# A gated recurrence followed by a low-rank mixer and an MLP: whole-batch loads, two chunks at a time, and fp32 weights cast on chip

## The chip, the cores and the metric

The kernel runs on one core of one Trainium2 chip. Its time is device microseconds of one execution, taken as the median of several runs. The profile is of a further execution, recorded by the hardware profiler. Six instruction streams matter: PE (TensorE, matmuls, with its weight loads PEld beside them), ACT (ScalarE), DVE (VectorE), POOL (GpSimd), and the queues from which transfers are issued, SP (SyncE) and POOL's own. All transfers run on the same 16 DMA engines.

## The reference

There are 4 batches, 8 heads, a sequence of 768 and a head of 48 columns; q, k, v and alpha are float32. Each head carries a state of 48 x 48 along the sequence:

```
state = alpha[t][:, None] * state + outer(k[t], v[t])
y[t]  = q[t] @ state
```

The heads' y, side by side, are x (768 x 384 for a batch), and then

```
xt = x.transpose(0, 2, 1)
h  = xt @ U @ V                        # U: 768 x 32, V: 32 x 768
u  = x + h.transpose(0, 2, 1)
out = u + relu(u @ w_ch1) @ w_ch2      # w_ch1: 384 x 1536, w_ch2: 1536 x 384
```

## The kernel before

Nothing is scheduled at run time. `Plan.add` collects operations, each with an engine, a cost in ns, what it reads and writes (`r`, `w`) and a priority. `Plan.run` then plays them through with those costs: at each step, of the operations that could start first, it takes the one with the lowest priority number, gives its `Buf`s the slot of their `Pool` that comes free first, and calls its function, which emits the instructions. So the order of each engine's stream is fixed when the kernel is built, and an engine that meets an instruction whose data is late waits with all that stands behind it.

The recurrence is computed by chunks of 128 steps, six to a batch, for all 8 heads at once (`stage_gla`, once per chunk). Heads go in four pairs, one of a pair on partitions 0 to 47 and the other from 64 on. The steps of a chunk, with their lines:

- four loads of 128 x 8 x 48 float32 from SP (L263): alpha, k, q, v, one chunk each, from a pool `io` of 40 slots. The innermost run in memory is one head's row of 48 numbers, 192 bytes;
- ACT takes the log of alpha into `lt` (L265), POOL casts v to bf16, `rv` (L267);
- PE forms the cumulative sum with a triangle of ones (L272) and its totals by head pair (L274);
- ACT takes exp of minus the sum, `ai` (L282), of the sum, `aa` (L283), and of the totals, `tot` (L284);
- POOL multiplies: `rk` = k times `ai` (L286), `rq` = q times `aa` (L287);
- PE transposes the four head pairs of each (L295), ACT (L304) and DVE (L306) copy them out of PSUM into `qk`;
- PE forms the scores (L321), DVE multiplies them with a triangular mask into `pm` (L332), once for each half of the heads;
- PE forms y from the state (L347) and from the masked scores (L352), and ACT copies it into `xb` (L363);
- PE adds the old state (L376) and the products of k and v (L381), DVE scales the sum with `tot` into the next state `st` (L389).

`stage_mix` does the low-rank part of a batch: x with U (L406), a copy (L414), V with that (L417), the sum into `ub` (L418), transposes (L427) and their copies into `uT` (L435). `mlp1` has two halves of 384 columns, 12 tiles of three products each (L447), with relu on ACT (L455) and DVE (L457) in turn. `mlp2` has, for each of the six chunks, 12 products (L471), the sum into `ou` (L478) and a store (L479).

The weights come by POOL's queue, cast to bf16 by the transfer: U (L245), four copies of V (L247), w_ch1 (L250) and w_ch2 (L253). The first two are issued behind the first chunk, the others behind the fourth and the fifth chunk of batch 0.

PSUM has eight banks: two pairs for scores and y (`pair`), two single ones (`gen`), and two for the MLP (`mlp`). The last batch's MLP may use all of them.

Of the kernel before, what the change touches and what calls it, by code (L numbers as in the profile page):

```python
# [14 lines left out]
class Pool:  # L15


    def __init__(self, slots):
        self.slots = list(slots)
        self.free = [0.0] * len(self.slots)  # L20


class Buf:


    def __init__(self, pool=None, slot=None):
        self.pools = pool if isinstance(pool, list) else ([pool] if pool else [])
        self.slot = slot
        self.home = None
        self.idx = 0  # L30
        self.left = 0
        self.last = 0.0
# [5 lines left out]
class Op:  # L38
    __slots__ = ("eng", "cost", "fn", "prio", "deps", "bufs", "n", "end", "users", "est", "i", "keep")


class Plan:


    LAT = {"PE": 230.0, "ACT": 120.0, "DVE": 120.0, "POOL": 150.0, "SP": 0.0, "DMA": 0.0}

    def __init__(self):
        self.ops = []
        self.writer = {}
        self.readers = {}  # L50

    def add(self, eng, cost, fn, r=(), w=(), prio=0.0, keep=(), after=()):
# [4 lines left out]
        op.keep = keep  # L57
# [14 lines left out]
        op.deps.update(x for x in after if x is not None)  # L72
        op.deps.discard(op)
        bufs = []
        for k in list(r) + list(w) + list(keep):
            b = k[0] if isinstance(k, tuple) else k
            if isinstance(b, Buf) and b not in bufs:
                bufs.append(b)
        op.bufs = bufs
        for b in bufs:  # L80
            b.left += 1
# [3 lines left out]
    def run(self):  # L85
# [12 lines left out]
        while todo:  # L98
            best = None
            for eng, cand in ready.items():  # L100
                now = clock.get(eng, 0.0)
                ok = []
                for op in cand:
                    t = op.est
                    for b in op.bufs:
                        if b.slot is None:
                            s = [x for p in b.pools for x in p.free if x is not None]
# [15 lines left out]
            for b in op.bufs:  # L123
                if b.slot is None:
                    _, n, x = min((f, n, x) for n, p in enumerate(b.pools) for x, f in enumerate(p.free) if f is not None)
                    p = b.pools[n]
                    p.free[x] = None
                    b.home, b.idx, b.slot = p, x, p.slots[x]
# [9 lines left out]
            for b in op.bufs:  # L138
                b.left -= 1
                b.last = max(b.last, op.end + self.LAT[eng])  # L140
                if b.left == 0 and b.home is not None:
                    b.home.free[b.idx] = b.last
# [18 lines left out]
def kernel(  # L161
# [22 lines left out]
    W = 112  # L184
    TW = S // 2

# [22 lines left out]
    vm_sb = const.tile([128, S], BF16, name="vm_sb")  # L209

    io = Pool(slots("io", 40, [C, H, D], FP32))
    lt_s = slots("lt", 3, [C, H, 64], BF16)
# [318 lines left out]
```

## Time and profile before

| | |
|---|---|
| median of 3 runs (lowest, highest) | 210.85 us (210.44, 213.79) |
| the profiled execution | 212.57 us |
| its span, first to last instruction | 210.8 us |
| mean granted TensorE clock | 0.992 |
| busy: PE / DVE / ACT / POOL | 174.7 / 97.4 / 91.3 / 60.8 us |
| read from HBM, written | 24.08 MB, 4.72 MB |
| packets under 512 bytes, of all | 101104 of 106244 |

The profile's page cuts the span into 40 equal slices and gives for each the busy tenths of an engine, the share of the DMA engines and what they moved in GB/s. A row of the timeline has a start and a duration in us, the engine, the line, the operation and the tiles (output, arrow, inputs), how many, and in brackets how long the engine stood idle before and what ended that. A row of the windows has a stretch and its length, then the busy time of PE, PEld, DVE, ACT and POOL (with the number of instructions), the granted clock, the DMA share and GB/s. A row of a chain has a start, a duration, and what the time was spent on. A row of the groups has, after the bar, the total busy time, the mean ns of one, and the idle time before the group with what ended it. Matmuls are pipelined and their ends modelled, so PE's busy time is more than its work.

### The profile page before, as it was taken

What the parts mean: (1) busy time and instruction counts of PE and PEld (TensorE: products, weight loads), DVE (VectorE), ACT (ScalarE), POOL (GpSimd) and SP (SyncE); (2) the same over time, 40 slices, a digit from 0 to 9 for tenths busy, and PEclk for the clock granted to TensorE, in tenths of its full rate; (3) what the DMA queues carried; (4) which work ended last, traced back from release to release, by engine and by line L of the source; (5) the groups of instructions that cost most, each with busy time, mean ns of one, the idle gap of its engine ahead of it and who ended that gap; (6) DMA issues with size and microseconds to landing.
All of it is one profiled execution on the core that took longest, in us unless ns stands there. A gap on an engine that the chain in (4) does not pass through costs nothing.

```text
span 210.8 us, 4417 instructions
## 1 busy us (share of the span) xinstructions
PE 174.7 (83%) x1732; PEld 107.5 (51%) x1732; DVE 97.4 (46%) x196; ACT 91.3 (43%) x209; POOL 60.8 (29%) x92
## 2 busy tenths in 40 slices
PE   1367868204899999899998499999999999999993
PEld 0245646001656655465665356565465656566561
DVE  1124526002657564766646557565542544433331
ACT  3255454003586654967465744643341450320100
POOL 8544663200074454435462830420000000000000
PEclk9999999999999999999999969999999999999999
DMA  7999999999999999999999950011102001212222
GB/s 127 179 188 190 165 190 178 189 190 173 192 168 197 164 195 156 198 174 196 171 212 159 222 164 2 3 37 37 40 0 99 13 3 37 75 40 75 75 74 77
DMA packets 106244, 26.48 MB, mean 126 GB/s; under 512 B 101104, under 2 KB 105840, under 8 KB 106224
## 3 DMA queue, kind: packets, MB, share of 16 engines
q1 hardware_dynamic: 103296, 23.60, 63.5%
q0 software_dynamic: 2928, 2.61, 7.8%
q8 instruction: 13, 0.21, 0.4%
q14 instruction: 7, 0.06, 0.1%
HBM read 24.08 MB, written 4.72 MB: 137 GB/s over the span
## 4 chain that ended last, share of the span: by engine, by line
PE 57%; DMA 16%; SPq 14%; ACT 3%; issue 3%; DVE 3%; POOL 1%; POOLq 0%; ACTq 0%
PE ps L471 21%; PE ps L447 20%; SPq L263 14%; DMA io<-in_alpha_dram 11%; DMA io<-in_v_dram 4%; PE ps L295 3%; PE ps L321 3%; PE ps L352 2%; PE ps L347 2%; DMA out_dram<-ou 2%; PE ps L427 2%; PE ps L417 2%; DVE ub L418 1%; PE ps L381 1%; PE ps L272 1%
## 5 line engine op out<-in xcount | busy, mean ns | idle before, releaser
L447 PE MATMUL ps<-uT,w_sb 128*128 128x384 bf16 x288 | 54.9, 329 | 0.5 <-ACT h1t L455 0.4
L471 PE MATMUL ps<-w_sb,h1t 128*128 128x384 bf16 x288 | 51.9, 326 | 0.0
L455 ACT ACTIVATE h1t<-ps 128x384 bf16<-128x384 f32 x48 | 23.4, 491 | 38.7 <-PE ps L447 38.6
L332 DVE TENSOR_TENSOR pm<-ps,maskc 128x512 bf16<-128x512 f32 x48 | 31.5, 685 | 18.8 <-PE ps L321 18.7
L471 PEld LDWEIGHTS <-h1t 128*128 128x128 bf16 x288 | 26.8, 97 | 16.4 <-issue 0.2
L447 PEld LDWEIGHTS <-w_sb 128*128 128x128 bf16 x288 | 26.2, 98 | 16.6 <-issue 2.2
L457 DVE TENSOR_SCALAR h1t<-ps 128x384 bf16<-128x384 f32 x48 | 26.2, 555 | 16.6 <-PE ps L447 16.0
L286 POOL TENSOR_TENSOR rk<-io,ai 128x384 bf16<-128x384 f32 x24 | 21.9, 913 | 37.6 <-ACT ai L282 35.2
L478 DVE TENSOR_TENSOR ou<-ub,ps 128x384 f32<-128x384 bf16 x24 | 13.3, 553 | 30.8 <-PE ps L471 27.8
L306 DVE COPY qk<-ps 128x512 bf16<-128x512 bf16 x24 | 10.1, 422 | 35.9 <-ACT utx L414 14.6
L265 ACT ACTIVATE lt<-io 128x384 bf16<-128x384 f32 x24 | 12.6, 524 | 32.5 <-DMA io<-in_alpha_dram 32.5
L267 POOL CAST rv<-io 128x384 bf16<-128x384 f32 x24 | 12.1, 503 | 38.6 <-DMA io<-in_v_dram 35.9
L287 POOL TENSOR_TENSOR rq<-io,aa 128x384 bf16<-128x384 f32 x24 | 21.9, 911 | 0.5 <-ACT tot L284 0.3
L304 ACT COPY qk<-ps 128x512 bf16<-128x512 bf16 x24 | 14.0, 583 | 13.0 <-PE ps L295 8.6
L321 PE MATMUL ps<-qk 48*128 48x128 bf16 x192 | 11.2, 247 | 5.3 <-ACT qk L304 3.4
L363 ACT CAST xb<-ps 128x384 bf16<-128x384 f32 x24 | 11.4, 477 | 9.4 <-PE ps L352 9.1
L352 PE MATMUL ps<-rv,pm 128*128 128x48 bf16 x192 | 13.8, 193 | 1.1 <-DVE pm L332 1.0
L282 ACT ACTIVATE ai<-ps 128x384 bf16<-128x384 f32 x24 | 11.9, 494 | 6.0 <-PE ps L274 5.0
L406 PE MATMUL ps<-xb,u_sb 128*32 128x384 bf16 x24 | 3.6, 376 | 12.8 <-ACT xb L363 11.6
L295 PEld LDWEIGHTS <-rq 128*128 128x128 bf16 x96 | 7.1, 108 | 13.6 <-issue 12.4
L418 DVE TENSOR_TENSOR ub<-xb,ps 128x384 bf16<-128x384 bf16 x24 | 12.4, 550 | 3.0 <-PE ps L417 2.6
L272 PE MATMUL ps<-lt,ut_ones 128*128 128x384 bf16 x24 | 9.1, 379 | 5.3 <-ACT lt L265 5.3
(44 smaller groups left out, 164.4 us busy)
## 6 DMA issues: line engine op xcount, KB each, us to landing
io<-in_alpha_dram SPq DMA_DIRECT2D x24, 192.0 KB, 4.5
io<-in_k_dram SPq DMA_DIRECT2D x24, 192.0 KB, 4.6
io<-in_q_dram SPq DMA_DIRECT2D x24, 192.0 KB, 4.4
io<-in_v_dram SPq DMA_DIRECT2D x24, 192.0 KB, 4.5
out_dram<-ou SPq DMA_DIRECT2D x24, 192.0 KB, 1.9
w_sb<-in_moe_w_ch_dram POOLq DMA_DIRECT2D x2, 1152.0 KB, 14.1
vm_sb<-in_moe_V_dram POOLq DMA_DIRECT2D x4, 48.0 KB, 5.2
u_sb<-in_moe_U_dram POOLq DMA_DIRECT2D x1, 48.0 KB, 5.4
```

Source lines behind the costliest of these rows:

```text
L263: P.add("SP", 960, lambda t=t, src=src: nc.sync.dma_start(t(), src[b, :, sl, :].rearrange("h t d -> t h d")), w=[t], prio=kk)
L286: P.add("POOL", 930, lambda: nc.gpsimd.tensor_tensor(rk()[:, :, 0:D], kt(), ai(), op=ALU.mult), r=[kt, ai], w=[rk], prio=pr + 2)
L287: P.add("POOL", 930, lambda: nc.gpsimd.tensor_tensor(rq()[:, :, 0:D], qt(), aa(), op=ALU.mult), r=[qt, aa], w=[rq], prio=pr + 2)
L304: nc.scalar.copy(qk()[:, o : o + HP, :], t[:, o : o + HP, :])
L321: nc.tensor.matmul(s2[:, par, p, :], lhsT=qk()[o : o + D, HP + p, :], rhs=qk()[o : o + D, p, :], start=(p == 0), stop=(p == HP - 1),)
L332: nc.vector.tensor_tensor(pm().rearrange("t (hp two) c -> t two hp c", two=2)[:, par], s2[:, par], maskc.to_broadcast([C, HP, C]), op=ALU. ...
L352: nc.tensor.matmul(y2[:, p, :], lhsT=pm()[:, 2 * p + par, :], rhs=rv()[:, 2 * p + par, :], start=(p == 0 and sprev is None), stop=(p == HP ...
L418: P.add("DVE", 550, lambda c=c, hb=hb: nc.vector.tensor_tensor(ub()[:, c, :], xb()[:, c, :], hb()[:, 0:DM], op=ALU.add), r=[hb, (xb, c)], ...
L447: nc.tensor.matmul(bank(hb)[:, 0:TW], lhsT=w1_sb[:, ct, jt * 128 : (jt + 1) * 128], rhs=uT()[:, ct, tt * TW : (tt + 1) * TW], start=(ct == ...
L455: P.add("ACT", 500, lambda jt=jt, hb=hb: nc.scalar.activation(h1()[:, jt, tt * TW : (tt + 1) * TW], bank(hb)[:, 0:TW], AF.Relu), r=[hb], w ...
L457: P.add("DVE", 560, lambda jt=jt, hb=hb: nc.vector.tensor_scalar_max(h1()[:, jt, tt * TW : (tt + 1) * TW], bank(hb)[:, 0:TW], 0.0), r=[hb] ...
L471: nc.tensor.matmul(bank(hb)[:, 0:DM], lhsT=h1()[:, jt, c * C : (c + 1) * C], rhs=w2_sb[:, jt, :], start=(jt == 0), stop=(jt == NJ - 1),)
```

## The change

- **Loads.** The four inputs come by whole batches (L308): 128 x 48 x 48 float32, 1.18 MB each, in a tile whose rows are 64 numbers wide, so that each run of 48 numbers lies 256 bytes behind the one before. The pool `io` has six such slots. There are 16 loads instead of 96; each still consists of 192-byte runs.
- **Weights.** They no longer come by POOL's queue. U (L275) and four copies of V (L277) are loaded in float32 from SP and cast by POOL (L278, L279). w_ch1 and w_ch2 come in three pieces each (L296), two to an `io` slot, and are cast by ACT or POOL (L270, L272), as a table says.
- **Pairs of chunks.** `stage_gla` works on two chunks at a time: logs, exponentials, products, casts and copies have twice the columns, scores are masked for both halves of the heads at once (L397), and three such steps make a batch. The recurrence over chunks remains: within a step a state is made for each chunk (L422, L429, L432).
- **Engines by hand for batch 0.** For the first batch a table says which engine does the product with k, that with q, the cast of v and the copy of the transposed q; for one chunk of the second and third step ACT copies the scores and POOL cuts the triangle out of them (L301) in place of DVE's mask; and the steps of this batch may also use the MLP's two banks. The later batches have POOL for products and casts, ACT and DVE for the copies.
- **Else.** `ub` is gone: the sum with the low-rank part is written over `xb`. `h1t` has three buffers of half a batch, `uT` two, `ou` three instead of four. The last batch's MLP takes any single bank. The plan's model of a transfer has other numbers.

```diff
-                clock[eng] = t + 450.0
-                dma = max(dma, t + 450.0) + op.cost
-                op.end = dma + 1800.0
+                clock[eng] = max(t + 450.0, dma)
+                dma = max(dma, t + 1200.0) + op.cost
+                op.end = dma + 1700.0
...
-    io = Pool(slots("io", 40, [C, H, D], FP32))
+    io = Pool(slots("io", 6, [C, H * NC, 64], FP32))
...
-    def load_weights():
-        nc.gpsimd.dma_start(u_sb, moe_U.rearrange("(c p) r -> p c r", p=128))
+    def load_low_rank():
+        P.add("SP", 450, lambda: nc.sync.dma_start(u_in, moe_U.rearrange("(c p) r -> p c r", p=128)), w=["u_in"], prio=0.3)
         for g in range(4):
-            nc.gpsimd.dma_start(vm_sb[32 * g : 32 * g + R, :], moe_V)
+            P.add("SP", 250, lambda g=g: nc.sync.dma_start(vm_in[32 * g : 32 * g + R, :], moe_V), w=[("vm_in", g)], prio=0.3)
+        P.add("POOL", 350, lambda: nc.gpsimd.tensor_copy(u_sb, u_in), r=["u_in"], w=["u"], prio=300)
+        P.add("POOL", 1000, lambda: nc.gpsimd.tensor_copy(vm_sb, vm_in), r=[("vm_in", g) for g in range(4)], w=["vm"], prio=300)
...
+        engs = ["ACT", "POOL", "POOL", "ACT", "POOL", "POOL"]
...
+            P.add("SP", 2000, lambda src=src, stage=stage: nc.sync.dma_start(stage(), src), w=[(t, i)], prio=0.5)
+            P.add(engs[i], cost[engs[i]], lambda dst=dst, stage=stage, e=engs[i]: copy(e, dst, stage()), r=[(t, i)], w=[("w1" if i < 3 else "w2", i % 3)], prio=400 + i)
...
+    def load(b):
+        ts = [Buf(io) for _ in range(4)]
+        for t, src in zip(ts, (alpha, k, q, v)):
+            P.add("SP", 4200, lambda t=t, src=src: nc.sync.dma_start(t()[:, :, 0:D], src[b].rearrange("h (c p) d -> p (h c) d", p=C)), w=[t], prio=b)
+        return ts
...
+        first = b == 0
+        win = 3 if first else 2
+        prs = pair0 if first else pair
+        ek = ("POOL", "DVE", "POOL")[g] if first else "POOL"
+        eq = ("DVE", "POOL", "DVE")[g] if first else "POOL"
+        ev = ("ACT", "POOL", "ACT")[g] if first else "POOL"
+        eqt = ("DVE", "DVE", "ACT")[g] if first else "DVE"
+        split = (-1, 1, 1)[g] if first else -1
...
+            if i == split:
+                P.add("ACT", 1150, lambda sc=sc, pmi=pmi: nc.scalar.copy(pmi().rearrange("t two hp c -> t (two hp c)"), sc().rearrange("p two c -> p (two c)")), r=[sc], w=[pmi], prio=pr + 1)
+                P.add("POOL", 1500, lambda pmi=pmi: f_tri(pmi), r=[pmi], w=[pmi], prio=pr + 1)
+            else:
+                P.add("DVE", 1230, f_mask, r=[sc], w=[pmi], prio=pr + 1)
```

What stands where, first on SP. Before, the loads go chunk by chunk (the tile names carry the slot):

```order
L263 DMA io0_82<-in_alpha_dram 128x8x48
L263 DMA io1_83<-in_k_dram 128x8x48
L263 DMA io2_84<-in_q_dram 128x8x48
L263 DMA io3_85<-in_v_dram 128x8x48
L263 DMA io4_86<-in_alpha_dram 128x8x48
```

Now the whole of batch 0 stands first, then the low-rank factors and the weights, then batch 1:

```order
L308 DMA io0_84<-in_alpha_dram 128x48x48
L308 DMA io1_85<-in_k_dram 128x48x48
L308 DMA io2_86<-in_q_dram 128x48x48
L308 DMA io3_87<-in_v_dram 128x48x48
L275 DMA u_in_82<-in_moe_U_dram 128x6x32
L277 DMA vm_in_83<-in_moe_V_dram 32x768 x4
L296 DMA io4_88<-in_moe_w_ch1_dram 128x3x512 x2
L296 DMA io5_89<-in_moe_w_ch1_dram 128x3x512
L296 DMA io5_89<-in_moe_w_ch2_dram 128x4x384
L296 DMA io0_84<-in_moe_w_ch2_dram 128x4x384 x2
L308 DMA io1_85<-in_alpha_dram 128x48x48
```

The first v was the fourth load and had the first chunk's 0.2 MB; it is still the fourth, with the whole batch's 1.18 MB, and the weights stand between the batches.

On DVE, in batch 0. Before, a chunk's masks (`pm`) and its state (`st`) follow one another:

```order
L306 COPY qk0_155<-ps_184 128x512
L389 TENSOR_TENSOR st0_161<-ps_184,tot0_151 112x192
L332 TENSOR_TENSOR pm0_158<-ps_184,maskc_74 128x4x128 x2
L306 COPY qk1_156<-ps_184 128x512
L332 TENSOR_TENSOR pm1_159<-ps_184,maskc_74 128x4x128
```

Now:

```order
L272 COPY qt0_126<-ps_150 128x1024
L272 COPY qt1_127<-ps_150 128x1024
L397 TENSOR_TENSOR pm0_129<-ps_150,maskc_74 128x1024
L397 TENSOR_TENSOR pm1_130<-ps_150,maskc_74 128x1024
L397 TENSOR_TENSOR pm3_132<-ps_150,maskc_74 128x1024
L432 TENSOR_TENSOR st0_133<-ps_150,tot0_119 128x192
L397 TENSOR_TENSOR pm0_129<-ps_150,maskc_74 128x1024
L432 TENSOR_TENSOR st1_134<-ps_150,tot0_119 128x192
```

Three masks of all eight heads stand ahead of the batch's first state, and a fourth ahead of the second.

On POOL, where the last batch begins. Before, it casts one chunk of v (`rv`) in each turn:

```order
L286 TENSOR_TENSOR rk1_129<-io31_113,ai1_150 128x8x48
L287 TENSOR_TENSOR rq2_127<-io32_114,aa1_148 128x8x48
L267 CAST rv0_142<-io4_86 128x384
L286 TENSOR_TENSOR rk2_130<-io30_112,ai0_149 128x8x48
L287 TENSOR_TENSOR rq0_125<-io39_121,aa0_147 128x8x48
```

Now the cast of batch 3's v (the first row of `rv1`, from slot 4) stands ahead of that batch's product with k (slot 3) and with q (slot 5):

```order
L355 TENSOR_TENSOR rq2_95<-io1_85,aa1_114 128x16x48
L272 CAST rv1_111<-io4_88 128x768
L355 TENSOR_TENSOR rk1_97<-io3_87,ai1_117 128x16x48
L355 TENSOR_TENSOR rq0_93<-io5_89,aa0_113 128x16x48
L355 TENSOR_TENSOR rk2_98<-io3_87,ai0_116 128x16x48
```

v is the last of a batch's loads, and the two products of the batch now stand behind its cast.

More of the change, by code (lines that the diff above doesn't have):

```diff
@@ L106, in run @@
                         if b.slot is None:
-                            s = [x for p in b.pools for x in p.free if x is not None]
+                            s = [f for f in map(b.pool.when, range(len(b.pool.slots))) if f is not None]
                             if not s:
@@ L140, in run @@
                 b.last = max(b.last, op.end + self.LAT[eng])
-                if b.left == 0 and b.home is not None:
-                    b.home.free[b.idx] = b.last
+                if b.left == 0:
+                    b.pool.give(b.idx, b.last)
             for u in op.users:
@@ L244, in load_weights @@
[L244 to L263 removed]
+    uts = Pool(slots("uT", 2, [128, NCT, S], BF16))
@@ L368, in stage_gla @@
[L368 to L377 removed]
+                        t[:, i * HP + p, :],
```

408 lines of the change are left out of this document (217 added, 191 removed).

## The prediction

> **What bounds the kernel now.** I read the slices of the page first, then the timeline around the hole in them, then rates by window, and last the chain that ended last.
>
> ```profile
> PE   1367868204899999899998499999999999999993
> DMA  7999999999999999999999950011102001212222
> GB/s 127 179 188 190 165 190 178 189 190 173 192 168 197 164 195 156 198 174 196 171 212 159 222 164 2 3 37 37 40 0 99 13 3 37 75 40 75 75 74 77
> ```
>
> A slice is 5.3 us. PE is loose for ten slices, stands still for one, then is full to the end. The transfers are full from the second slice to the 23rd (some 124 us). So there are two stages: up to 57 us PE waits for data; after it PE works, on what the transfers allow.
>
> ```profile
> 44.59 0.50 POOL L267 CAST rv<-io 128x384 bf16<-128x384 f32 x1 [6.29 <-DMA io<-in_v_dram]
> 49.21 0.52 ACT L265 ACTIVATE lt<-io 128x384 bf16<-128x384 f32 x1 [12.32 <-DMA io<-in_alpha_dram]
> 50.15 0.48 PE L406 MATMUL ps<-xb,u_sb 128*32 128x384 bf16 x1 [11.63 <-ACT xb L363]
> 57.06 0.32 PE L447 MATMUL ps<-uT,w_sb 128*128 128x384 bf16 x1
> ...
> 31.80 8.73 SPq L263 DMA_DIRECT2D io<-in_k_dram  x1
> 40.57 4.86 SPq L263 DMA_DIRECT2D io<-in_q_dram  x1
> 45.48 3.55 SPq L263 DMA_DIRECT2D io<-in_v_dram  x1
> ```
>
> The hole: from 31.8 to 49 us SP is held at three loads in a row (8.73, 4.86 and 3.55 us to issue one) while the weights, casting transfers of POOL's queue, share the 16 transfer engines with them. v of a late chunk comes at 44.6 us, alpha of the next at 49.2, and the MLP of batch 0 (L447) begins only at 57.06.
>
> ```profile
> 2.50:3.25 0.75, 0.00 (x0) 0.00 (x0) 0.00 (x0) 0.00 (x0) 0.75 (x2) 1.00 1.26 255
> 47.00:48.00 1.00, 0.00 (x0) 0.00 (x0) 0.00 (x0) 0.00 (x0) 0.00 (x0) 1.00 1.26 243
> 98.00:99.00 1.00, 1.00 (x17) 0.63 (x14) 0.69 (x2) 0.59 (x3) 1.00 (x2) 1.00 1.25 239
> 99.00:104.00 5.00, 5.00 (x72) 3.26 (x71) 2.60 (x6) 2.52 (x7) 2.90 (x4) 1.00 1.41 190
> 60.00:125.00 65.00, 59.95 (x745) 36.95 (x744) 39.79 (x80) 40.82 (x101) 32.14 (x44) 0.99 1.11 186
> 190.00:200.00 10.00, 10.00 (x63) 6.04 (x62) 3.26 (x6) 0.98 (x2) 0.00 (x0) 1.00 0.22 79
> ```
>
> The last columns are transfer share and GB/s. Loads in 192-byte pieces run at 186 GB/s over a long stretch (190 in a steady part), but at 239 to 255 for about a microsecond after a pause. Stores of 1,536-byte rows moved 79 GB/s at a share of 0.22: 359 GB/s if full.
>
> ```profile
> 161.53 11.70 PE ps L447 x72
> 100.14 0.20 PE ps L352 x4
> 100.86 0.21 PE ps L381 x8
> 103.33 0.33 PE ps L321 x8
> 104.21 0.16 PE ps L272
> 104.38 0.08 PE ps L274 x4
> 107.94 0.22 PE ps L295 x4
> 109.44 0.28 PE ps L406 x4
> 207.40 0.55 DVE ou L478
> 127.00:147.00 20.00, 20.00 (x251) 12.07 (x248) 12.32 (x26) 9.67 (x22) 3.53 (x4) 1.00 0.06 21
> ```
>
> From the chain PE's work can be priced: 0.1625 us for an MLP product (11.70/72), so 23.4 us for a batch's 144; a chunk of the recurrence takes about 2.1 (cumulative sum 0.24, eight transposes 0.45, scores 0.33, y 0.7 to 0.8 at 0.20 for four, state 0.3 to 0.4), the low-rank stage 2.6. In all some 38 us a batch, 151 for four. The stretch from 127 to 147 us has no load left in it and granted clock 1.00; its matmuls, so priced, make 0.95 of the time. The end costs 3.4 us after the last matmul (207.40 to 210.8). The span is 210.8 us, the execution 212.57, the median of the runs 210.85: I sum spans and take them for the median.
>
> **The change, part by part.** Let T be the time of one input tensor of one batch, 1.18 MB. It is the unknown on which nearly all hangs, as the trace has no load in this form (whole batch, rows of 192 bytes put down every 256 bytes). Bounds: 6.3 us at 186 GB/s, 4.6 at 255; outside them 7.2 at the worst busy slice (164), 3.3 at the stores' 359. I take 246 GB/s, the mean of 255, 243 and 239, so T = 4.8: these rows show what the engines do with such pieces, and what seems to push them down, many small transfers, gets rarer (96 loads become 16). That the share is higher (1.41) at 190 than at 239 says that pieces wait for one another when slow. The long row speaks for 6.3 and is kept for the range.
>
> By the Trainium skill, DMA: Bandwidth & Descriptors, "How a descriptor splits into AXI transactions", a piece that does not begin on a 256-byte boundary costs extra beats; rows packed every 192 bytes need 9 beats on average, rows every 256 bytes 6, so if writes are the limit the sum would have 190 x 9/6 = 285 GB/s (estimate from that page), T = 4.1, and end at 182. The trace agrees only in part: packed rows went at 239 too. Against the change speaks the same page's "Specifications": below 512 bytes no line rate, and the pieces stay at 192; by that, T = 6.3 and no gain.
>
> *Batch 0.* The order on SP is alpha, k, q, v, U, V, six weight pieces.
>
> ```profile
> 3.86 0.52 ACT L265 ACTIVATE lt<-io 128x384 bf16<-128x384 f32 x1 [1.85 <-DMA io<-in_alpha_dram]
> L265 ACT ACTIVATE lt<-io 128x384 bf16<-128x384 f32 x24 | 12.6, 524 | 32.5 <-DMA io<-in_alpha_dram 32.5
> L435 ACT COPY uT<-ps 128x768 bf16<-128x768 bf16 x12 | 9.4, 799 | 9.0 <-PE ps L427 9.0
> L286 POOL TENSOR_TENSOR rk<-io,ai 128x384 bf16<-128x384 f32 x24 | 21.9, 913 | 37.6 <-ACT ai L282 35.2 <-PE ps L471 2.3
> L267 POOL CAST rv<-io 128x384 bf16<-128x384 f32 x24 | 12.1, 503 | 38.6 <-DMA io<-in_v_dram 35.9 <-PE ps L295 2.4 <-PE ps L447 0.2
> L332 DVE TENSOR_TENSOR pm<-ps,maskc 128x512 bf16<-128x512 f32 x48 | 31.5, 685 | 18.8 <-PE ps L321 18.7
> L389 DVE TENSOR_TENSOR st<-ps,tot 112x192 bf16<-112x192 f32 x20 | 7.1, 353 | 4.8 <-PE ps L381 4.7
> masks.py:199 POOL TENSOR_SCALAR_AFFINE_SELECT ident<-ident 128x128 bf16<-128x128 bf16 x1 | 0.3, 292 | 0.1
> ```
>
> The first chunk's alpha (0.2 MB, 0.8 us at 246) was in use at 3.86 us: 3.0 us lie around a transfer, and v is there at 3.0 + 4T = 22.2. Logs, exponentials, rk, rq, transposes and scores lie under the loads of k, q and v. After v: the cast of v (0.8, as ACT's 768 columns), three masks that stand ahead of the first state on DVE (2 x 0.685 each, the first about when v lands, 4 us), another mask, five states in a row at about 1.05 each (0.35 on DVE and products and handovers), last y and its copy: some 10 us. Then the low-rank stage, 6.9 us today (50.15 to 57.06): MLP at v + 17, 39 us, against 57.06. The hand-set split keeps other work off this chain: copies on ACT, and a triangle on POOL at between 0.3 and 2.3 us (one or eight of the 128-column row). New are the weight casts: 1,536 columns, 2.0 us on POOL (4 x 0.503), about 1.5 on ACT, four and two of them. One of ACT's stands ahead of two copies of y and is in the 10; POOL's end about when the MLP wants them. If that cover were gone, 2 to 4 us. POOL no longer issues transfers, worth nothing: its queue was not in the chain. The weights are now 4.72 MB at 359 GB/s, 13.1 us, and U and V 1.5; today they take the loads from 32 to 49 us.
>
> *Later batches.* A batch needs four T on the one queue. The slots (six) do not stop it where I follow it: each is read out a few microseconds after landing, the ones for batch 1 while the weights land. v of batch 1 is there at 3.0 + 4T + 14.6 + 4T = 17.6 + 8T; before v of batch 2 come two stores (0.55 each), before v of batch 3 three: 18.7 + 12T and 20.35 + 16T, i.e. 56, 76 and 97 us. These stores wait on DVE with loads behind them on SP, but the loads ahead still keep the engines busy: nothing. Three store buffers for four: nothing, though the third store of batch 0 stands behind v of batch 2 on SP; its buffer is free about 5 us before its next use, and that margin shrinks with nothing but a faster PE.
>
> PE takes its work in a fixed order, so the places where it needs v of a batch matter: in the new order 121, 102 and 80 us of priced work are left there for batches 1, 2, 3. For batch 3: 399 MLP products 64.8, 84 transposes 4.8, scores 2.0, y 3.8, states 1.9, sums 0.5, low rank 2.2. On POOL, the cast of v (1.0) and rk (2 x 0.913) stand between: 2.9 us.
>
> **Sum.** By batch 3: 97.2 + 2.9 + 80.1, 2.0 for PE's loss in the mixed stretch (5% of some 40 us), 3.4 for the end: **186 us**. By PE alone from 39.2: 137.1 of work, 5 lost, 3.4: 185. Both are nearly equal, so a faster T gains 4 us per us of T, a slower one costs 16. The two-chunk tiles halve instructions on ACT, DVE and POOL, which wait on the chain only in batch 0: nothing more.
>
> **The rivals.**
> - *Write-limited rows:* packed rows were what slowed the loads, and they go with the short service of the first row (255 GB/s at a share of 1.26) and as many in flight as the long row has (1.41): 255 x 1.41/1.26 = 285 GB/s, T = 4.1. The kernel is then PE's from batch 0 on: 3.0 + 16.4 + 17 + 137.1 + 5 + 3.4 = 182 us. For it: the share rises while the rate falls, so pieces wait for one another somewhere; against it: the same packed rows at 255. The Trainium skill's count of beats (DMA: Bandwidth & Descriptors), above, speaks for this case.
> - *The new form changes nothing in the rate:* T from 5.4 to 6.65. PE is earlier at the MLP (45 us) and then waits for batches 1, 2 and 3: at 6.3, 20.35 + 100.8 + 88.4 = 210 us; at 5.6, 198. For it: 65 us on end at 186 GB/s, whatever the engines did; against it: no long stretch of one transfer has been seen.
> - *Slower:* whole-batch pieces, 16 engines drifting apart over 48 rows a partition, go no better than the worst slices (164 GB/s), T = 7.2: 20.35 + 115.2 + 88.4 = 224 us. It decides from T = 6.65 on (178 GB/s, 215 us). For it: every third slice shows 154 to 174; against it: the slices beside them make 190.
>
> **How the numbers follow.** T from 4.45 to 5.35 (183 to 194 us): 0.42. Write-limited: 0.25. Unchanged rate: 0.24, of which 0.13 below 206.6 us and 0.11 within 2% (what a measurement here can tell from none). Slower: 0.09. So faster 0.80, same 0.11, slower 0.09. The likeliest is 186; range 177 (write-limited with a shorter chain after v, 5 us less) to 208 (T = 6.2); its own range is 180 to 195.
>
> **What would show it.** Loads at 240 GB/s or more and the four of batch 0 landed by 22 us; the MLP's first product near 39; PE full from there with short waits for loads; no load after 97 us; 88 us from v of batch 3 to the end. Wrong: loads at 190 (PE then waits for k, q and v of batches 1 to 3, time about 210), an MLP start past 45 us with the loads on time (the chain on DVE or ACT is longer), or PE waiting on DVE or ACT after 100 us.

## The result, and the profile after

The changed kernel takes 189.44 us (188.06 to 192.66), the one before it 212.05 on the same chip: a ratio of 0.8935 [0.881, 0.9059]. The profiled execution took 188.06, with a span of 186.4 us against 210.8. The profile of one experiment, that with 70 and 40 added matmuls, was taken in a disturbed execution, so its span isn't used.

The slices of the page, now of 4.7 us each:

```profile
PE   0156889789989997999998999999999999999992
DMA  4899999969899887899890010101020011212122
GB/s 115 242 268 276 226 345 383 356 189 253 256 255 288 242 234 203 247 271 260 251 271 27 0 46 0 46 9 44 35 86 0 4 42 42 86 46 84 51 78 84
```

The hole in PE's row (before, the ninth slice, from 42 us on) is gone, no slice between the fourth and the last is under seven tenths, and the loads go at about 250 GB/s instead of 180 to 190. They end in the 22nd slice, at 99 us; before, at 124.

Landings are read from the timeline, where POOL casts v (with what it waited for), and two rows of PE and DVE mark the MLP's start and the last output:

```profile
21.27 0.82 POOL L272 CAST rv<-io 128x768 bf16<-128x768 f32 x1 [2.12 <-DMA io<-in_v_dram]
38.81 1.14 PE L519 MATMUL ps<-uT,w_sb 128*128 128x384 bf16 x6
56.33 2.36 POOL L272 CAST rv<-io 128x768 bf16<-128x768 f32 x3 [1.49 <-DMA io<-in_v_dram]
77.40 0.82 POOL L272 CAST rv<-io 128x768 bf16<-128x768 f32 x1 [2.90 <-DMA io<-in_v_dram]
98.60 0.82 POOL L272 CAST rv<-io 128x768 bf16<-128x768 f32 x1 [9.88 <-DMA io<-in_v_dram]
182.84 0.55 DVE ou L545
```

v of the four batches comes at 21.3, 56.3, 77.4 and 98.6 us (forecast: 22.2, 56, 76, 97.2), the MLP starts at 38.8 (39.2).

By windows (length, then busy time of PE, PEld, DVE, ACT, POOL, granted clock, transfer share, GB/s), with batch 0's loads, the weights, a later stretch of loads, and all from the MLP's start to the last product:

```profile
2.50:21.00 18.50, 8.10 (x78) 6.08 (x79) 5.26 (x5) 9.66 (x15) 6.78 (x5) 1.00 0.92 260
25.00:35.00 10.00, 8.88 (x143) 5.91 (x141) 3.22 (x7) 7.07 (x9) 5.77 (x5) 1.00 1.05 382
57.00:97.00 40.00, 38.11 (x584) 25.23 (x583) 27.89 (x44) 25.23 (x40) 17.02 (x14) 1.00 0.87 250
38.81:182.84 144.03, 138.80 (x1443) 86.10 (x1440) 78.57 (x131) 68.22 (x115) 37.57 (x28) 1.00 0.42 125
```

The MLP starts 18.2 us sooner (57.06 to 38.81); from there to the end of the span it is 147.6 us against 153.7. These two make the 24.4. From the MLP's start on PE stands still for 5.2 us in 144. One line of the page was not foreseen:

```profile
DMA packets 32067, 29.07 MB, mean 156 GB/s; under 512 B 1584, under 2 KB 30768, under 8 KB 32048
```

Before it was

```profile
DMA packets 106244, 26.48 MB, mean 126 GB/s; under 512 B 101104, under 2 KB 105840, under 8 KB 106224
```

The 16 tensors have 98,304 rows of 192 bytes; before, each was a packet, and now four share one: the trace has 24,576 packets of 768 bytes. In the compiled program a whole-batch load reads 768 bytes at a time, four time steps of one head, and lays them down as rows of four neighbouring partitions; a load of one chunk reads 192 at a time.

### The profile page after: what moved, and what is told of

It is laid out like the page before. It is cut to its first block, busy times and chain, and to the rows that moved or that the text cites. A ratio compares the mean times of both kernels' runs of the same rounds, so it can differ in the third digit from the quotient of the medians.

```text
span 186.4 us, 4083 instructions
## 1 busy us (share of the span) xinstructions
PE 162.0 (87%) x1728; PEld 102.8 (55%) x1728; DVE 95.2 (51%) x160; ACT 90.6 (49%) x144; POOL 54.5 (29%) x51
## 2 busy tenths in 40 slices
DMA packets 32067, 29.07 MB, mean 156 GB/s; under 512 B 1584, under 2 KB 30768, under 8 KB 32048
## 4 chain that ended last, share of the span: by engine, by line
PE 47%; DMA 20%; SPq 19%; POOL 4%; DVE 4%; issue 3%; ACT 1%; POOLq 0%; DVEq 0%
PE ps L538 20%; PE ps L519 17%; SPq L308 13%; DMA io<-in_v_dram 11%; DMA io<-in_k_dram 9%; SPq L296 3%; POOL rk L355 3%; SPq L275 2%; PE ps L364 2%; DVE xb L491 1%; PE ps L387 1%; PE ps L500 1%; DVE pm L397 1%; PE ps L455 1%; PE ps L422 1%
## 5 line engine op out<-in xcount | busy, mean ns | idle before, releaser
L397 DVE TENSOR_TENSOR pm<-ps,maskc 128x1024 bf16<-128x1024 f32 x22 | 26.5, 1219 | 5.5 <-PE ps L387 4.2
L355 POOL TENSOR_TENSOR rk<-io,ai 128x768 bf16<-128x768 f32 x11 | 18.7, 1709 | 31.7 <-DMA io<-in_k_dram 16.4
L545 DVE TENSOR_TENSOR ou<-xb,ps 128x384 f32<-128x384 bf16 x24 | 13.3, 553 | 28.3 <-PE ps L538 28.1
L270 ACT COPY kt<-ps 128x1024 bf16<-128x1024 bf16 x12 | 12.1, 1013 | 13.8 <-PE ps L364 11.3
L355 POOL TENSOR_TENSOR rq<-io,aa 128x768 bf16<-128x768 f32 x10 | 17.1, 1718 | 5.2 <-ACT kt L270 3.6
L491 DVE TENSOR_TENSOR xb<-xb,ps 128x384 bf16<-128x384 bf16 x24 | 12.5, 550 | 6.2 <-PE ps L490 5.9
L508 ACT COPY uT<-ps 128x768 bf16<-128x768 bf16 x12 | 9.5, 800 | 8.2 <-PE ps L500 8.1
L467 ACT CAST xb<-ps 128x768 bf16<-128x768 f32 x12 | 9.6, 800 | 6.8 <-PE ps L455 6.6
L272 POOL CAST rv<-io 128x768 bf16<-128x768 f32 x10 | 8.0, 822 | 16.4 <-DMA io<-in_v_dram 16.4
L331 ACT ACTIVATE lt<-io 128x768 bf16<-128x768 f32 x12 | 9.8, 845 | 5.7 <-DMA io<-in_alpha_dram 5.7
L432 DVE TENSOR_TENSOR st<-ps,tot 128x192 bf16<-128x192 f32 x20 | 7.1, 354 | 7.6 <-PE ps L429 6.5
L349 ACT ACTIVATE ai<-ps 128x768 bf16<-128x768 f32 x12 | 9.8, 814 | 1.8 <-PE ps L341 1.7
```

The source lines that it names most:

```text
L270: nc.scalar.copy(dst, src)
L331: P.add("ACT", 800, lambda: nc.scalar.activation(lt()[:, :, :, 0:D], ch(at), AF.Ln), r=[at], w=[lt], prio=pr + 4)
L355: ENG[eng].tensor_tensor(dst()[:, :, :, 0:D], ch(src), fac().rearrange("t g (h d) -> t g h d", d=D), op=ALU.mult)
L397: nc.vector.tensor_tensor(pmi().rearrange("t two hp c -> t (two hp) c"), sc().rearrange("p two (hp c) -> p (two hp) c", c=C), maskc.to_bro ...
L491: P.add("DVE", 550, lambda c=c, hb=hb: nc.vector.tensor_tensor(xb()[:, c, :], xb()[:, c, :], hb()[:, 0, 0:DM], op=ALU.add), r=[hb, (xb, c) ...
L545: P.add("DVE", 550, lambda: nc.vector.tensor_tensor(ou(), xb()[:, c, :], hb()[:, 0, 0:DM], op=ALU.add), r=[hb, (xb, c)], w=[ou], prio=100)
```

## Experiments: what makes the loads faster

The prediction hangs on T, the time of a tensor, and the change alters two things at once that bear on it: the pitch of the rows (256 bytes instead of 192) and the size of a transfer. In the compiled programs the input tiles begin 32 bytes past a multiple of 256. A row at a pitch of 256 then stays inside one stretch of 256 bytes (a line, below); of rows at a pitch of 192 three in four cross from one line into the next.

**The pitch alone, in the kernel before** (and 36 slots instead of 40, for room).

```diff
-    io = Pool(slots("io", 40, [C, H, D], FP32))
+    io = Pool(slots("io", 36, [C, H, 64], FP32))
...
-            P.add("SP", 960, lambda t=t, src=src: nc.sync.dma_start(t(), src[b, :, sl, :].rearrange("h t d -> t h d")), w=[t], prio=kk)
+            P.add("SP", 960, lambda t=t, src=src: nc.sync.dma_start(t()[:, :, 0:D], src[b, :, sl, :].rearrange("h t d -> t h d")), w=[t], prio=kk)
...
```

> The kernel before, with one thing of the change: each 48-number row of a load is put down every 256 bytes (io tiles 64 numbers wide, 36 slots in place of 40 for room). Theory A, the pitch gives the rate: packets are no longer 192 bytes, the loads run at 240 GB/s or more over long stretches, they end near 100 us in place of 124, and the MLP starts some 5 us sooner; 198 to 205 us. Theory B, the size of a transfer gives the rate: 192-byte packets, 186 GB/s, 209 to 214 us.

204.23 us, ratio 0.9758 [0.9695, 0.9821]. The same window, of the kernel before and of this one:

```profile
2.50:21.00 18.50, 9.84 (x110) 6.76 (x109) 4.53 (x9) 8.00 (x20) 9.99 (x16) 1.00 1.24 190
```

```profile
2.50:21.00 18.50, 11.11 (x130) 7.70 (x130) 5.75 (x12) 8.68 (x22) 11.28 (x17) 1.00 1.12 207
```

From 190 to 207 GB/s, with as many packets as before: the pitch helps a little here. The time is in theory A's range, but its reason does not hold: the packets stayed at 192 bytes, and 240 GB/s were not reached.

**Packed rows in the changed kernel.** The tiles are used with a pitch of 192 bytes; all else stays.

```diff
+    def rows(t):
+        return t().rearrange("p a w -> p (a w)")[:, 0 : H * NC * D].rearrange("p (a d) -> p a d", d=D)
...
-            P.add("SP", 4200, lambda t=t, src=src: nc.sync.dma_start(t()[:, :, 0:D], src[b].rearrange("h (c p) d -> p (h c) d", p=C)), w=[t], prio=b)
+            P.add("SP", 4200, lambda t=t, src=src: nc.sync.dma_start(rows(t), src[b].rearrange("h (c p) d -> p (h c) d", p=C)), w=[t], prio=b)
...
```

> The changed kernel with its rows packed every 192 bytes again, in the same whole-batch transfers; nothing else moves. Theory A (pitch): T goes back to about 6.3 us (186 GB/s), PE waits for k, q and v of batches 1 to 3, v of batch 3 near 125 us and the end at 205 to 213 us. Theory B (size): 768-byte packets stay, T 4.5, 186 to 192 us.

217.01 us, ratio 1.0352 [1.0276, 1.0429]: slower than before the change. Its window, and its last v:

```profile
2.50:21.00 18.50, 4.77 (x46) 3.24 (x46) 0.96 (x1) 7.46 (x12) 4.36 (x4) 1.00 1.01 191
```

```profile
126.06 0.82 POOL L272 CAST rv<-io 128x768 bf16<-128x768 f32 x1 [15.54 <-DMA io<-in_v_dram]
```

The packets are as few as in the changed kernel (32,067), yet the rate is that of the kernel before. That is theory A, with a time above its 205 to 213 us. So large transfers and few packets bring nothing by themselves, and neither do pairs, weights and table while the loads go at this rate. The prediction's sum holds here too: 126.06 + 2.9 + 80.1 + 2 + 3.4 = 214.5, and the span is 215.3.

**Padded rows in small transfers.** Chunk by chunk again, with pitch, table and order of the tensors kept.

```diff
+        for g in range(NC // G):
+            for t, src in zip(ts, (alpha, k, q, v)):
+                def go(t=t, src=src, g=g):
+                    for c in range(g * G, (g + 1) * G):
+                        dst = t().rearrange("p (h c) w -> p c h w", c=NC)[:, c, :, 0:D]
+                        nc.sync.dma_start(dst, src[b, :, c * C : (c + 1) * C, :].rearrange("h p d -> p h d"))
...
```

> The changed kernel with the padded tiles, the engine table and the order kept, but every tensor loaded chunk by chunk again, pair after pair: per pair of chunks two transfers of 8 rows of 192 bytes per partition for each of the four tensors, 96 transfers instead of 16. First theory (small packets keep the padded rows at about 205 GB/s, as in the kernel before with padded tiles): 5.75 us for each tensor's worth, v of batch 0 complete near 26 us but its first pair near 11, MLP start at 36 to 41 us, v of batch 3 near 115, span 200 to 206, loads set the end. Rival (it is only the count of what is in flight, and the padded rows run at 250 to 260 GB/s in this form too): the first pair's work begins near 9 us instead of 17, the MLP starts at 32 to 36, and the span comes to 180 to 184, faster than the changed kernel: whole-batch loads would then cost time at the start.

202.86 us, ratio 0.9622 [0.9576, 0.9669], 107,075 packets.

```profile
2.50:21.00 18.50, 9.00 (x119) 7.08 (x119) 7.07 (x9) 7.54 (x12) 4.43 (x5) 1.00 1.06 209
```

The first theory held, in the rate and in the span (200.6). With the three runs ahead of it this makes a table of two by two:

| GB/s in 2.5 to 21 us | a row to a packet | four rows to a packet |
|---|---|---|
| packed | 190 | 191 |
| padded | 207, 209 | 260 |

Neither half alone gives the gain. It looks like the slower of two limits: one of small packets near 208, one of packed rows near 191. Whether the first comes from the packets or from the short reads that make them, no run parts.

**What is wrong with packed rows.** Two runs move the padded rows within their 256 bytes.

```diff
-            P.add("SP", 4200, lambda t=t, src=src: nc.sync.dma_start(t()[:, :, 0:D], src[b].rearrange("h (c p) d -> p (h c) d", p=C)), w=[t], prio=b)
+            P.add("SP", 4200, lambda t=t, src=src: nc.sync.dma_start(t()[:, :, 16 : 16 + D], src[b].rearrange("h (c p) d -> p (h c) d", p=C)), w=[t], prio=b)
...
```

> The changed kernel with one thing moved: the rows of 48 values go to columns 16 to 63 of the 64 of an input tile instead of 0 to 47. The tiles begin 32 bytes past a multiple of 256, so a row of 192 bytes now lies from byte 96 to byte 288 and every row crosses a multiple of 256; in the changed kernel none does, in the run with packed rows three of four do. Pitch, packets, work and order stay. Theory A (what slows a load is a row that crosses a 256-byte line): about 190 GB/s or less in the stretches where loads are alone, 6.3 us or more for each tensor, v of batch 3 at 121 us or later, span 209 to 220 us. Theory B (the cost grows with the 32-byte pieces that a row is cut into, here 9, against 7 in the changed kernel and 10 on average in the packed one): 5.9 us for each tensor, some 205 GB/s, v of batch 3 near 115, span 202 to 206. Theory C (it is only that packed rows stand back to back, and a gap between them is what helps): 255 GB/s as in the changed kernel, span 186 to 189.

```diff
+    gap = const.tile([128, 56], FP32, name="gap")
+    nc.vector.memset(gap, 0.0)
     io = Pool(slots("io", 6, [C, H * NC, 64], FP32))
```

> The changed kernel with a tile of 224 bytes a partition, which nothing reads, put ahead of the input tiles, so that each input row begins at a multiple of 256 bytes instead of 32 past one. Theory A (crossing is what costs): no row crossed before either, so the loads stay at 250 to 260 GB/s and the span at 186 to 188. Theory B (cost by 32-byte pieces, 6 instead of 7 in a row, and aligned ones): 280 to 300 GB/s, v of batch 0 near 19.5 us instead of 21.3, v of batch 3 4 to 10 us earlier than 98.6; the span comes to 183 to 186, since the MLP's start moves by at most 2 us and TensorE has 137 us of work from there.

229.7 us, ratio 1.0885 [1.0851, 1.0919], and 190.71, ratio 0.9069 [0.9007, 0.913]. Their windows, in this order:

```profile
2.50:21.00 18.50, 3.73 (x38) 2.37 (x37) 0.96 (x1) 6.64 (x11) 2.67 (x3) 1.00 1.06 168
```

```profile
2.50:21.00 18.50, 7.87 (x74) 5.85 (x75) 5.02 (x5) 9.66 (x15) 6.79 (x5) 1.00 0.91 257
```

Every row across a line: 168 GB/s, slower even than packed rows (191), of which only three in four cross. None across: 257 and 260, whether a row begins on a line or 32 bytes behind. That is theory A, and in numbers: a quarter of the rows at 260 and three quarters at 168 make 1 / (0.25/260 + 0.75/168) = 184, near the 191 of the packed run. Theory B wanted 9 pieces of 32 bytes to go better than 10 and 6 better than 7; theory C wanted 255. Both fell. A's time was too mild (228.3 for 209 to 220), since it had taken the rate of packed rows.

## Experiments: the weights, the table, and what sets the end

**Weights by POOL's casting transfers**, as before the change, behind POOL's first cast of v.

```diff
...
+    def load_w1():
+        nc.gpsimd.dma_start(w1_sb, moe_w_ch1.rearrange("(c p) f -> p c f", p=128))
...
+        if kk == 1:
+            for i, (f, w) in enumerate(((load_weights, ["u", "vm"]), (load_w1, [("w1", j) for j in range(3)]), (load_w2, [("w2", j) for j in range(3)]))):
+                P.add("POOL", 1000, f, w=w, prio=0.1 * i, after=[P.writer[rv]])
...
-            load_low_rank()
-            load_big()
```

> The changed kernel with the weights loaded as before: cast by the transfer, from POOL's queue, issued right behind POOL's first cast of v of batch 0 (the same place in time as in the change). The casts on ACT and POOL fall away. Theory: the casting transfers are what made the hole, they take longer than 13 us and hold up the loads of batch 1, so the MLP starts later than 38.8 us (43 to 50) and v of batch 1 comes later than 56; 193 to 202 us. Rival, the queue does not matter as all share the same engines and bytes: 186 to 191 us.

197.59 us, ratio 0.9426 [0.9357, 0.9496]. A step of its chain of waits, and three rows of PE:

```profile
25.43 22.12 DMA io<-in_q_dram
```

```profile
39.95 1.04 PE L378 MATMUL ps<-ident,rk 128*128 128x128 bf16 x8 [5.33 <-POOL rk L369]
49.37 1.04 PE L378 MATMUL ps<-ident,rq 128*128 128x128 bf16 x8 [4.81 <-POOL rq L369]
53.32 1.14 PE L533 MATMUL ps<-uT,w_sb 128*128 128x384 bf16 x6
```

A hole is back: q of batch 1 takes 22 us beside the weights, PE stands for 5.33 and 4.81 us at products of batch 1 that its order puts ahead of batch 0's low-rank stage, and the MLP starts at 53.3. The span (195.2) is only 8.8 longer than 186.4; part of batch 1's work on PE is done by then. The time was forecast, but not its reason, that v of batch 1 would come later than at 56:

```profile
52.45 2.37 POOL L272 CAST rv<-io 128x768 bf16<-128x768 f32 x3
```

It is cast at 52.45, sooner than the 56.33 of the changed kernel, and the weights' last packet had ended at 47.2. So these transfers do not bring the data later. The loss lies in the order: the plan counts 1 us for issuing each group of them and nothing for their sharing the engines with the loads, and lets PE meet batch 1 too early. What they would cost with another order, no run shows.

**No table for batch 0.**

```diff
-        first = b == 0
+        first = False
```

> The changed kernel with batch 0 treated like the others: products with k and q and the cast of v all on POOL, masks all on DVE, no third bank pair. Theory that the loads set the end (v of batch 3 at 98.6 us and what follows): the MLP starts 3 to 6 us later, but the end moves by less than 2 us, 186 to 191 us. Rival, PE's own work from the MLP's start sets it: the end moves by all of the delay, 191 to 195 us.

201.08 us, ratio 0.959 [0.9521, 0.9659], span 199.4. v of batch 0 is there at 21.5 as before, the MLP starts at 50.57. Rows of POOL and ACT:

```profile
33.60 1.63 POOL L355 TENSOR_TENSOR rk<-io,ai 128x768 bf16<-128x768 f32 x1
35.20 1.64 POOL L355 TENSOR_TENSOR rq<-io,aa 128x768 bf16<-128x768 f32 x1
...
42.12 0.84 ACT L331 ACTIVATE lt<-io 128x768 bf16<-128x768 f32 x1 [4.24 <-DMA io<-in_alpha_dram]
42.87 0.78 ACT L467 CAST xb<-ps 128x768 bf16<-128x768 f32 x1
```

With only two pairs of banks, the third step starts when the first has given its pair back; its products stand on POOL at 33.6, between weight casts, where the changed kernel had them at 12.5 to 20 on POOL and DVE. Then ACT waits for batch 1's alpha with the last copy of y behind it. The delay of 11.8 us reaches the end whole (13.0), though no load is late (v of batch 3 is cast at 97.04): loads do not set the end. That is more than either expectation. The table's parts were taken away together; which of them counts most is read from these rows only.

**Less to load**, in the same order on every engine. k, q and v of batches 1 to 3 bring 12 rows of 48; those batches compute on partly old data.

```diff
+            n = 48 if b == 0 or src is alpha else 12
```

> The changed kernel with less to load and the same instruction order on every engine: of k, q and v of batches 1 to 3 only 12 of the 48 rows of a partition are transferred (the rest of the tile is what an earlier transfer left there, so those batches compute on mixed data); alpha and batch 0 are whole. From the MLP's start at 38.8 us the changed kernel has 136.8 us of TensorE work and loses 7.2 us, and then 3.5 us pass to the end. First theory (after the MLP's start TensorE's own work sets the end, and the loads cost what TensorE loses while it waits for k and v of batches 1 to 3): v of batch 3 lands before 80 us instead of 98.6, the loss falls from 7 to 3 to 5 us, the span is 181 to 184. Rival (the loads set the end, as the prediction's sum has it: v of batch 3, then 2.9 and 80 us): the end moves with the landing, by 10 us or more, to a span of 176 or less.

185.34 us, ratio 0.8803 [0.874, 0.8867], span 183.1.

```profile
38.48:179.59 141.11, 138.78 (x1443) 86.05 (x1440) 78.34 (x131) 68.04 (x115) 37.58 (x29) 1.00 0.26 72
```

```profile
79.31 1.25 SPq L309 DMA_DIRECT2D io<-in_v_dram  x1
```

The window runs from the MLP's start to the last product; the second row is SP's issue of the last v, at 79.3, so that it lands some 15 us sooner than at 98.6 (4.1 us pass from issue to landing). Yet the end moves by 3.3 only. PE's work from the MLP's start is the same 138.8; its idle time falls from 5.2 to 2.3 us. At 260 GB/s the later loads cost 3 us in all, and the rest is PE's.

**Stores of batch 0 from POOL.**

```diff
+        if b == 0:
+            P.add("POOL", 550, lambda: nc.gpsimd.dma_start(out[b, c * C : (c + 1) * C, :], ou()), r=[ou], prio=-1)
...
```

> The changed kernel with the six stores of batch 0 issued by POOL instead of SP, so that none of them stands between the loads of later batches on SP's queue. First theory (the loads still share in setting the end: SP waits up to 4.4 us for an output tile before it can issue the next load): the DMA share from 57 to 97 us rises from 0.87, v of batch 3 lands 3 to 5 us before 98.6, and the span falls by 2 to 3 us to 183 to 185. Second theory (from the MLP's start on TensorE's own 137 us of work set the end, with 7 us lost all told): v of batch 3 lands 3 to 5 us earlier as well, but the span stays within 1 us of 186.4; POOL pays for six issues, which could make it up to 1 us longer.

196.09 us, ratio 0.9265 [0.9208, 0.9321], span 192.7. Neither theory had that. The transfer share from 57 to 97 rose to 0.94, but the last v came at 98.5, no sooner. That hides a gain: v of batch 1 had come later, at 58.5 instead of 56.3, so the eight loads after it took 40.0 us instead of 42.3. The loss is elsewhere; PE, and two windows:

```profile
55.56 0.62 PE L364 MATMUL ps<-ident,rq 128*128 128x128 bf16 x8 [2.52 <-POOL rq L355]
...
57.72 1.04 PE L387 MATMUL ps<-qt,kt 48*128 48x128 bf16 x16
...
101.72 1.03 PE L364 MATMUL ps<-ident,rk 128*128 128x128 bf16 x8 [2.58 <-POOL rk L355]
```

```profile
53.30:56.71 3.41, 1.15 (x13) 0.89 (x14) 0.76 (x2) 0.26 (x2) 2.81 (x3) 1.00 0.98 273
57.00:60.00 3.00, 3.00 (x24) 1.50 (x23) 1.63 (x2) 0.20 (x1) 2.32 (x3) 0.50 0.91 251
```

Twice PE waited 2.5 us for POOL, and with each wait the granted clock went to 0.50 for 3.4 us (from 56.7 and from 101.1): 24 matmuls from 57 to 60 us, where the changed kernel has 55 at 1.00. Neither wait is for a store: in the first POOL itself stood 2.48 us for q of batch 1, before its first store at 55.45, and in the second its product stood behind two casts of batch 3's v, which was there at 98.48. From its MLP's start on, the changed kernel's longest wait of PE is this, and no lower clock follows it:

```profile
74.56 0.62 PE L364 MATMUL ps<-ident,rq 128*128 128x128 bf16 x8 [1.02 <-POOL rq L355]
```

**Keeping PE busy in batch 0.** In the changed kernel eight transposes take 1.03 us in batch 0 and 0.62 later. Matmuls of the identity were put ahead of the first sums (72) and of the first step's transposes (24):

```diff
+            for i in range(72 if kk == 0 else 0):
+                nc.tensor.matmul(cb()[:, 0, 128 * (i % 4) : 128 * (i % 4 + 1)], lhsT=ident, rhs=ident, start=True, stop=True)
...
+            for i in range(24 if kk == 0 and src is rk else 0):
+                nc.tensor.matmul(tb()[:, 0, 128 * (i % 4) : 128 * (i % 4 + 1)], lhsT=ident, rhs=ident, start=True, stop=True)
```

> The changed kernel with 96 matmuls of the identity by itself added to TensorE where it waits in batch 0, 72 ahead of the first cumulative sums and 24 ahead of the first transposes, into banks that the next instruction overwrites; the order of everything else is the same. In the changed kernel eight transposes start to start take 0.97 us in batch 0 (from 21.59) and 0.45 from 50.79, and TensorE stood idle for over 7 us before its first matmul. In the run with stores from POOL two idle stretches of 2.5 us were each followed by some 3.5 us at a granted clock of 0.50. First theory (an idle stretch leaves TensorE at half speed until it has been busy some us; kept busy it runs at full speed in batch 0): eight transposes in 0.45 to 0.6 us by 22 us, and since the chain from v to the MLP is five dependent steps of TensorE and VectorE, the MLP's start moves from 38.8 to 34 to 37 and the span to 182 to 185. Rival (TensorE's speed in batch 0 is not what the chain waits for, or the gaps between are long enough to slow it again): start at 38 to 41, span 186 to 189.

and then 70, with 40 right behind the sums:

```diff
+            for i in range(40 if kk == 1 and src is rk else 0):
```

> The changed kernel with 110 matmuls of the identity by itself: 70 ahead of the first cumulative sums, and 40 right behind the last of these, ahead of the transposes that TensorE comes to first in batch 0. In the run before it the first filling worked (a cumulative sum took 0.32 us instead of 0.48), but then TensorE stood idle for 2.92 us until 13.74 and ran at half speed from about 14 to 39 us; its second filling stood behind that gap. First theory (the gap is what undoes the filling; without a gap of 2.5 us or more TensorE keeps full speed): eight transposes take 0.45 to 0.62 us at 22 us, the five state steps 0.7 to 1.0 us each instead of 1.32, the MLP starts at 34.5 to 37 instead of 38.8, and the span is 182 to 184.5, under the changed kernel's 186.4 by about as much as the start moves. Rival (shorter gaps between 14 and 22 us slow TensorE as well, or the chain waits for VectorE and ACT): start at 38 to 40, span 186 to 189.

190.9 us, ratio 0.9063 [0.898, 0.9146], and 190.79, ratio 0.9004 [0.894, 0.9068]: no gain. From the second, PE and a window:

```profile
8.50 0.32 PE L341 MATMUL ps<-lt,ut_ones 128*128 128x384 bf16 x1 [0.43 <-ACT lt L331]
...
14.90 0.62 PE L368 MATMUL ps<-ident,rk 128*128 128x128 bf16 x8 [0.88 <-POOL rk L357]
16.62 1.01 PE L368 MATMUL ps<-ident,rk 128*128 128x128 bf16 x8 [1.10 <-ACT kt L270]
```

```profile
20.00:36.00 16.00, 13.42 (x205) 9.55 (x204) 8.79 (x15) 9.82 (x11) 6.96 (x7) 0.50 0.99 323
```

The filling worked (a sum in 0.32 us, transposes in 0.62) until 16 us. From 13.1 to 16.5 us PE was busy for only 1.24, with waits of 0.5 to 1.1 us between short bursts; then the clock was at 0.50, up to the MLP at 39.1. Every execution of this kernel has a mean clock of 0.91 to 0.94. The rival was right. Whether a chain at full clock would be shorter was not reached, and stays open.

**One column of the table.**

```diff
-        ev = ("ACT", "POOL", "ACT")[g] if first else "POOL"
+        ev = ("POOL", "ACT", "ACT")[g] if first else "POOL"
```

> The changed kernel with one column of the engine table altered: v's casts of batch 0 by POOL, ACT, ACT instead of ACT, POOL, ACT. In the changed kernel v landed at 21.27, POOL cast the second pair's at once, and ACT cast the first pair's only at 23.57, behind the copy of transposed q; the five state steps began at 24.46. The order written by the planner changes with it. First theory (the first pair's v is the head of the chain to the MLP): the first state product begins at 22 to 23, the MLP 1 to 2 us earlier than 38.8, span 184 to 186. Rival (the masks on DVE, busy from 21.34 to 24.83, hold the state chain anyway): the MLP starts within 0.7 us of 38.8, span 186 to 188.

194.3 us, ratio 0.919 [0.9067, 0.9313], span 192.4. The first state product begins at 23.71 instead of 24.46 and the MLP at 38.22: the rival. That the end is 6 us later is put down to the order, which the planner wrote anew; no run parts it from the rest. One place where time goes:

```profile
85.83 0.80 PE L490 MATMUL ps<-utx,vm_sb 128*128 128x384 bf16 x2 [1.59 <-ACT utx L487]
```

```profile
81.23:84.64 3.41, 2.25 (x55) 1.43 (x52) 2.85 (x4) 0.50 (x2) 0.93 (x2) 1.00 0.98 302
84.64:91.47 6.83, 5.63 (x47) 3.38 (x47) 2.94 (x6) 5.49 (x9) 3.09 (x2) 0.50 0.71 211
```

PE waits 1.6 us for ACT and has a clock of 0.50 for 6.8 us. The wait did not bring the clock down: that fell at 84.64, 0.4 us after the wait began, behind 3.4 us in which PE had been busy for 2.25.

No run that does all the work beat the changed kernel.

## Why the prediction was right, point by point

- **Time per tensor.** 4.8 us forecast; (21.27 − 3.0) / 4 = 4.6 in batch 0, then (98.6 − 56.33) / 8 = 5.3 with the stores, for which the sum had (97.2 − 56) / 8 = 5.15. The size was right, the reason not. It was said that the pieces stay at 192 bytes and that fewer transfers help. They went four to a packet, and that alone is worth nothing (191 GB/s). The rate comes from rows that stay inside a line of 256 bytes, together with the shared packets. So the likeliest number, 186, was met with some luck: nothing in its reasons asked where the tiles begin.
- **Write-limited rows**, a rival at 182 us, had the right place and the wrong measure: it wanted 285 GB/s, and 257 to 260 were measured, with rows of six and of seven pieces of 32 bytes alike. The Trainium skill (DMA: Bandwidth & Descriptors, "How a descriptor splits into AXI transactions") cuts a descriptor, one piece of a transfer, at multiples of 256 bytes. The number of transactions that this makes of a row, 1, 1.75 and 2 (worked out from that page), has the order of the measured 260, 191 and 168; the number of beats, 7, 10 and 9, does not. The prediction's 6 and 9 beats hold for tiles that begin on a multiple of 256; here they begin 32 bytes past one.
- **Unchanged rate** (210 us) and **slower** (224) are what comes out with other addresses of the same rows: spans of 215.3 and 228.3. Here they did not hold, but the place of the rows decided it (64 bytes further on each crosses a line), not the size of the loads.
- **Batch 0.** v at 22.2, start at 39.2: measured 21.3 and 38.8. The length from v, 17 us, was right (17.5), though the trace has PE in it at half its later speed. The low-rank stage, 6.9 of the 17, was taken over from the kernel before, where it ran at that speed for the most part (full clock is on record there from 54.8 us).
- **The table** was the term most under-sized: the only price that the prediction had for it was 2 to 4 us, if the cover were gone. Without the whole table the start is 11.8 us later and the span 13.0.
- **Weights.** 13.1 us at 359 GB/s: 382 measured, right. Loaded the old way the span was 8.8 us longer, through PE's order and not through later data.
- **The sum.** Both routes came near: 97.2 + 2.9 + 80.1 + 2.0 + 3.4 by the loads, 39.2 + 137.1 + 5 + 3.4 by PE. Measured for the second: 38.8 + 138.8 + 5.2 + 3.6 = 186.4 (forecast for the last two: 5 and 3.4). "Nearly equal" was right, and PE's is the one that counts: with v of batch 3 some 15 us sooner 3.3 us were gained (forecast: 4 us for each us of T at first, then PE's floor).
- **Stores** were put at nothing. From v of batch 1 to v of batch 3 the loads took 42.3 us with batch 0's stores between them on SP and 40.0 with these on POOL, so some 2 us of load time, one profile each; as PE sets the end, that is not seen in the span.
- **The hole** was read as one slice after ten loose ones; PE's row has its zero in the ninth slice, and the stall of 11.63 us ends at 50.15. Nothing in the sum hangs on it.

## What to carry to other kernels

When a load of short rows is slow, look at where each row falls in on-chip memory before making transfers larger: give the rows a pitch and a start at which none crosses a multiple of 256 bytes, then let several share a packet, and measure both. And when PE's own work sets the end, a few microseconds of it standing still cost more than the wait: look at the granted clock behind each. Where an experiment writes the order of the engines anew, as several did here, its time is that of the order too.

## What the runs showed of the hardware

- Rows of 192 bytes load at 260 GB/s when none crosses a 256-byte line, 191 when three in four do, 168 when all do; and at 207 to 209, padded, with a packet for each row.
- TensorE's granted clock changes, in every trace here, at distances of 3.41 us or a multiple of it. Of 24 falls to 0.50 in these runs, 22 followed such a step in which PE was busy for half of the time or less (1.15 us with the wait of 2.52 us, 1.24 among the short bursts), two a step with PE busy for 0.55 and 0.66 of it; three steps with shares of 0.42 to 0.47 were followed by no fall. The Trainium skill (TensorE: Matmul & The Clock Gate, "Part 1") tells of a gate to half the clock after an idle window of about 3.4 us; here shorter waits did it.
- A clock of 1.00 in a view can mean that none is on record. The changed kernel's first record is at 37.7 us, that of the kernel before at 54.8; ahead of them the views show 1.00, while eight transposes take 1.03 us in the changed kernel's batch 0 and 0.62 later.
- Two products with k take POOL 4.00 us where DVE does one at their start, and 3.25 where it does none (3.23 in the run without the table, at the same place):

```profile
12.46 0.96 DVE L355 TENSOR_TENSOR rk<-io,ai 128x768 bf16<-128x768 f32 x1 [10.51 <-DMA io<-in_k_dram]
12.50 4.00 POOL L355 TENSOR_TENSOR rk<-io,ai 128x768 bf16<-128x768 f32 x2 [9.63 <-DMA io<-in_k_dram]
...
47.01 3.25 POOL L355 TENSOR_TENSOR rk<-io,ai 128x768 bf16<-128x768 f32 x2 [6.81 <-DMA io<-in_k_dram]
```
